# Sixteen transposes of the last pair moved from TensorE to transposing transfers on SyncE's queue

## The chip, the cores and the metric

The kernel runs on one core of one Trainium2 chip. The metric is the device time of one execution in microseconds (us), the median of several runs. Beside the times there is one profiled execution, taken by the hardware profiler. The engines are called PE (TensorE), DVE (VectorE), ACT (ScalarE), POOL (GpSimd) and SP (SyncE, which here only issues transfers).

## The reference

Gated linear attention as a recurrence over time, and then a two-layer MLP with a cosine gate, on its output:

```python
batch, n_heads, seq, head_dim = (4, 8, 768, 48)
for t in range(S):
    state = alpha[:, :, t, :, None] * state + einsum('bhd,bhe->bhde', k[:, :, t], v[:, :, t])
    y[:, :, t] = einsum('bhd,bhde->bhe', q[:, :, t], state)
x = y.transpose(0, 2, 1, 3).reshape(3072, 384)
h = x @ w_in            # 384 -> 2048
out = (h * cos(h)) @ w_out   # 2048 -> 384
```

All inputs and the output are float32; the kernel works in bf16 inside its products.

## The kernel before

The 3072 tokens are cut into twelve "pairs" J = 0..11 of 256 tokens, three for each of the four batches. Within a pair the 128 partitions hold 128 positions, and e = 0, 1 picks the even or the odd token of a position, so each partition has two tokens. The recurrence is computed in chunks of 64 positions: within a chunk as a masked score product, between chunks through a state.

For each pair the attention goes through these steps:

- `load` (L111) brings alpha, k, q and v in, each one transfer issued by SP.
- `ln` (L148), `cums` (L161 to L178) and `exps` (L200, L201) turn alpha into the decays cp and their inverses icp.
- `scale_k` (L206) and `scale_q` (L210) multiply k by icp and q by cp, giving kh and qh in bf16, on POOL for the late pairs. Each head takes 64 columns there, 48 of them used, so that two heads make 128 columns.
- `trans` (L236) transposes kh and qh on PE, in 128x128 blocks of two heads: for each e four blocks of kh and four of qh, so sixteen in a pair. They go to one PSUM tile T_ps per e, and `evict_T` (L242) copies that to the SBUF tile qkT, on DVE.
- `scores` (L252) multiplies, for each e, the transposed k of this e with the transposed q of both e, into two PSUM tiles A_ps. `mask` (L258) on DVE moves them to A_sb.
- `outer` (L270), `add_state` (L284) and `decay_state` (L292) carry the state on.
- `yT` (L329) forms the transposed output from A_sb, v, the state and the transposed q, and `evict_y` (L336) copies it to xT.

The MLP of a pair follows. `mlp1` (L346, the step m1) makes four blocks u of h in PSUM, two buffers of h_ps in turn; `cosine` (L352) on ACT and `gate` (L357) on DVE make gsb from each; `mlp2` (L366, the step m2) makes two halves of the output, each in four parts of four matmuls, and `evict_o` (L371) copies each half out of PSUM. Each half is stored by two transfers (L375), on SP but for the very last, from one of four buffers o_sb.

The order of the work is not that of the loops. Every piece is a `step` with an engine, a length, the steps that it needs, a rank and the buffers that it takes and gives. A planner in the kernel (L516 to L610) plays the steps through with these lengths and writes them out in the order of their planned starts; each engine then executes its own instructions strictly in that order. The lengths in the steps are the planner's numbers and not measurements. The planner also puts matmuls on zeros (`idle`, L384) into early gaps of PE.

The planner has a list DMAT of pairs whose transposes are planned as transfers, as one step per e on an engine "DMA", with a length of its own. It is empty before the change:

```python
if J in DMAT:
    step(("evT", J, e), "DMA", 2.0, [("sk", J, e), ("sq", J, e), ("yT", J - 2)],
         lambda J=J, e=e: trans_dma(J, e), r + RK["trans"], [("qkT", 1)] if e == 0 else [])
```

The step of the scores needs ("evT", J, 0) and ("evT", J, 1) in either form. A step on "DMA" is taken as usable some 2 to 3.5 us after its planned end.

Of the kernel before, what the change touches and what calls it, by code (L numbers as in the profile page):

```python
# [10 lines left out]
BF = mybir.dt.bfloat16  # L11
# [5 lines left out]
def kernel(  # L17
# [10 lines left out]
    nc = tc.nc  # L28
    B, H, S, D = q.shape
    DM, DF = moe_w_in.shape  # L30
    C = 128
# [4 lines left out]
    NP = H // 2  # L36
# [7 lines left out]
    NL, NQ, NV = 4, 3, 3  # L44
    BUF = {"a": 4, "in": 3, "cp": 3, "vb": 3, "qkT": 3, "A": 2, "un": 4, "us": 2, "c": 3, "xT": 3, "g": 4}

    consts = ctx.enter_context(tc.tile_pool(name="consts", bufs=1))
    sb = ctx.enter_context(tc.tile_pool(name="sb", bufs=2))
# [31 lines left out]
    lna_t, qh_t, kh_t, vz_t = [], [], [], []  # L80
    for r in range(NL):
        t = consts.tile([C, 2, H, 64], BF, tag=f"lna{r}", name=f"lna{r}")
        nc.vector.memset(t[:, :, :, D:64], 0.0)
        lna_t.append(t)
    for r in range(NQ):
        t = consts.tile([C, 2, H, 64], BF, tag=f"qh{r}", name=f"qh{r}")
        nc.vector.memset(t[:, :, :, D:64], 0.0)
        qh_t.append(t)
        t = consts.tile([C, 2, H, 64], BF, tag=f"kh{r}", name=f"kh{r}")
        nc.vector.memset(t[:, :, :, D:64], 0.0)  # L90
        kh_t.append(t)
    for r in range(NV):
        t = consts.tile([C, 2, NP, 2, 32], BF, tag=f"vz{r}", name=f"vz{r}")
# [7 lines left out]
    w1 = consts.tile([C, KT, DF], BF, tag="w1", name="w1")  # L101
    w2 = consts.tile([C, NF, DM], BF, tag="w2", name="w2")

    a_sb, kqv, cp_sb, icp_sb, vb_sb, qkT_sb, A_sb, c2_sb = {}, {}, {}, {}, {}, {}, {}, {}
# [88 lines left out]
    def exps(J, e):  # L193
        act_set("exp")
        w = HD + 2 * NP * e
        icp_sb[J, e] = sb.tile([C, HD], FP, tag=f"icp{e}", name="icp", bufs=BUF["cp"])
        if (J, e) not in cp_sb:
            cp_sb[J, e] = sb.tile([C, w], FP, tag=f"cp{e}", name="cp", bufs=BUF["cp"])
        t = cums_ps[J, e] if (J, e) in cums_ps else cp_sb[J, e]
        nc.scalar.activation(out=icp_sb[J, e], in_=t[:, 0:HD], func=AF.Exp, scale=-1.0)  # L200
        nc.scalar.activation(out=cp_sb[J, e], in_=t[:, 0:w], func=AF.Exp)  # L201
# [30 lines left out]
    def trans(J, e):  # L232
        T_ps[J, e] = ps.tile([C, 2 * NP, C], BF, tag="sh", name="T_ps", bufs=3)
        for i, x in ((1, kh_t[J % NQ]), (0, qh_t[J % NQ])):
            for p in range(NP):
                nc.tensor.transpose(T_ps[J, e][:, i * NP + p, :],  # L236
                                    x[:, e, 2 * p : 2 * p + 2, :].rearrange("s h d -> s (h d)"), ident_bf)

    def evict_T(J, e, copy):
        if J not in qkT_sb:  # L240
            qkT_sb[J] = sb.tile([C, 2, 2 * NP, C], BF, tag="qkT", name="qkT", bufs=BUF["qkT"])
        copy(out=qkT_sb[J][:, e], in_=T_ps.pop((J, e)))  # L242
# [145 lines left out]
    steps = {}  # L388

    def step(name, eng, length, deps, fn, rank, take=(), give=()):  # L390
        steps[name] = (eng, length, [d for d in deps if d is not None], fn, rank, take, give)
# [14 lines left out]
    HOLD = 0.29  # L406
    FULL = [0, 1, 2]
    WARM = 5.0
    DMAT = []
    copies = {"DVE": nc.vector.tensor_copy, "ACT": nc.scalar.copy, "POOL": nc.gpsimd.tensor_copy}  # L410
    mults = {"DVE": nc.vector, "POOL": nc.gpsimd}
    blk = {J: n for n, Js in enumerate(BLOCKS) for J in Js}
# [20 lines left out]
    for J in range(NJ):  # L433
# [13 lines left out]
        for e in range(2):  # L447
            if J in FULL:
                src = ("cums", J) if e else ("cums0", J)
            else:  # L450
                src = ("sub", J)
            step(("exps", J, e), "ACTe", 1.0, [src, ("exps", J, 0) if e and J in FULL else None],
                 lambda J=J, e=e: exps(J, e), rb, [], [("h" if J in FULL else "sh", 1)] if e else [])
            eng = SCALE.get((J, "k", e), "POOL")
            step(("sk", J, e), eng, 1.0 if eng == "POOL" else 0.9, [("exps", J, e), ("ld", "k", J)],
                 lambda J=J, e=e, eng=eng: scale_k(J, e, mults[eng]), r + RK["sk"] + e,
                 [("qk", 1)] if e == 0 else [], [("in_k", 1)] if e else [])
            eng = SCALE.get((J, "q", e), "POOL")
            step(("sq", J, e), eng, 1.0 if eng == "POOL" else 0.9, [("exps", J, e), ("ld", "q", J), ("sk", J, 0)],
                 lambda J=J, e=e, eng=eng: scale_q(J, e, mults[eng]), r + RK["sq"] + e, [], [("in_q", 1)] if e else [])  # L460
            eng = EVT.get((J, e), "DVE")
            if J in DMAT:
                step(("evT", J, e), "DMA", 2.0, [("sk", J, e), ("sq", J, e), ("yT", J - 2)],
                     lambda J=J, e=e: trans_dma(J, e), r + RK["trans"], [("qkT", 1)] if e == 0 else [])
            else:
                step(("trans", J, e), "PE", 0.45, [("sk", J, e), ("sq", J, e), ("yT", J - 2) if J > 1 else None],
                     lambda J=J, e=e: trans(J, e), r + RK["trans"], [("sh", 1)])
                step(("evT", J, e), eng, 0.72 if eng == "DVE" else 1.1, [("trans", J, e)],
                     lambda J=J, e=e, eng=eng: evict_T(J, e, copies[eng]), r + RK["evT"],
                     [("qkT", 1)] if e == 0 else [], [("sh", 1)])  # L470
            step(("scores", J, e), "PE", 0.33, [("evT", J, 0), ("evT", J, 1), ("scores", J, 0) if e else None],
                 lambda J=J, e=e: scores(J, e), r + RK["scores"], [("sh", 2)])
            for a in range(2):
                step(("mask", J, e, a), "DVE", 0.69,
                     [("scores", J, e), ("mask", J, e, 0) if a else (("mask", J, 0, 1) if e else None)],
                     lambda J=J, e=e, a=a: mask(J, e, a), r + RK["mask"], [("A", 1)] if a + e == 0 else [], [("sh", 1)])
# [42 lines left out]
    HOP = 0.2  # L519
# [3 lines left out]
    mode, end, order = "e", {}, []  # L523
# [20 lines left out]
    while avail:  # L544
        cands = {}
        cur = undone[0] if undone else []
        for name, dep in avail.items():
            eng, length, deps, fn, rank, take, give = steps[name]
            t = buffers(take)
            if t is None:  # L550
                continue
            t = max(t, dep)
            extra = 0.0
            if eng in ("ACTe", "ACTs"):
                begun = any(("ln", J) in end for J in cur)
                if eng == "ACTe":
                    if name[1] not in cur or (not begun and sins and rank > sins[0]):
                        continue
                    if mode == "s" and not begun:
                        if not all(("ln", J) in avail for J in cur):  # L560
                            continue
                        t = max([t] + [avail["ln", J] - 1.0 for J in cur])
                elif mode == "e" and begun:
                    continue
                if eng[3] != mode:
                    extra = 1.3
            e = eng[:3] if eng[:3] == "ACT" else eng
            cands.setdefault(e, []).append((max(t, free_at[e]), rank, name, extra))

        pick = None  # L570
        for e, cs in cands.items():
            s0 = min(cs)[0]
            c = min((c for c in cs if c[0] <= s0 + (HOLD if c[2][1] in EARLY else NEAR)), key=lambda c: (c[1], c[0]))
            if pick is None or c[0] < pick[0]:
                pick = c + (e,)
        s, rank, name, extra, e = pick
        eng, length, deps, fn, _, take, give = steps[name]
        avail.pop(name)
        if eng in ("ACTe", "ACTs"):
            mode = eng[3]  # L580
        if eng == "PE" and s < WARM:
            length *= 1.9
        end[name] = s + extra + length
        if name[0] == "sin":
            sins.remove(rank)
        if name[0] == "exps":
            n = BLOCKS.index(cur)
            logs_left[n] -= 1
            if logs_left[n] == 0:
                undone.pop(0)  # L590
        free_at[e] = end[name] if e != "X" else 0.0
        for buf, n in take:
            slots[buf][1] += n
        for buf, n in give:
            f, nt, ng = slots[buf]
            for i in range(n):
                f[(ng + i) % len(f)] = end[name]
            slots[buf][2] += n
        for kind in (name, ("start", name)):
            for u in users.get(kind, []):  # L600
                need[u] -= 1
                if need[u] == 0:
                    t = 0.0
                    for d in steps[u][2]:
                        if d[0] != "start":
                            far = steps[d][0][:3] != steps[u][0][:3]
                            t = max(t, end[d] + (HOP if far else 0.0) + ((3.5 if d[1][0] == "w" else 2.0) if steps[d][0] == "DMA" else 0.0))
                    avail[u] = t
        order.append((s, len(order), fn, name))
    assert len(order) == len(steps)  # L610
# [42 lines left out]
```

## Time and profile before

| what | value |
|---|---|
| median of 3 runs | 201.83 us (201.4 to 202.19) |
| the profiled execution | 202.26 us |
| its span, first to last instruction | 200.5 us |
| PE busy | 187.4 us, 93% of the span |
| DVE, ACT, POOL busy | 128.7, 130.2, 92.2 us |
| transposes L236, 192 matmuls | two groups of 96 (kh and qh), 219 ns each in the records, overlapping |
| evictions L242 on DVE | 23, mean 686 ns |
| transfers issued by SP: loads | 48, 384 KB each, 5.3 to 6.2 us to landing (medians of the four kinds) |
| transfers issued by SP: stores | 47, 96 KB each, 2.2 us to landing (median) |

Busy time is the time in which an engine has at least one instruction at work; matmuls are pipelined, so a record of 219 ns does not mean that PE gives one transpose in 219 ns. The chain of work that ended last goes back from the last instruction, at each step to what released it, and so tells which work set the end. On SP the page counts no busy time; its timeline has the instructions that issue transfers, and for how long each held SP.

### The profile page before, as it was taken

The numbers are of one execution on the slowest core, as the hardware profiler recorded it, in microseconds if no ns is written. First come the engines' busy times: TensorE is split into PE (matmuls) and PEld (weight loads), VectorE is DVE, ScalarE is ACT, GpSimd is POOL, SyncE is SP. The second block draws the span as 40 slices with busy tenths as digits, with TensorE's granted clock in tenths as the row PEclk, the third lists the DMA queues.
The fourth block names the chain that finished last, engine by engine and source line by source line (L and its number), as shares of the span: only waits on it lengthen the run. The fifth ranks groups of instructions, "written<-read, shape, count | busy, mean of one in ns | idle before, by whom it ended". The sixth has DMA issues, their size and how long they took to land.

```text
span 200.5 us, 6778 instructions
## 1 busy us (share of the span) xinstructions
PE 187.4 (93%) x2977; PEld 139.0 (69%) x2977; DVE 128.7 (64%) x185; ACT 130.2 (65%) x174; POOL 92.2 (46%) x144
## 2 busy tenths in 40 slices
PE   7889897789999899799999999999999999999990
PEld 7777785566767667568767767777777677687750
DVE  7384585478757756656867776768668578744341
ACT  3521674567796796796887887887878873365520
POOL 4496685138339465749285474165343531000000
PEclk9999999999999999999999999999999999999998
DMA  6999999978996799195819547120110110110203
GB/s 155 261 246 255 258 194 223 208 180 193 264 260 157 165 270 252 38 272 146 207 44 244 129 115 183 23 58 5 43 43 2 41 43 3 39 43 3 67 11 80
DMA packets 57502, 27.18 MB, mean 136 GB/s; under 512 B 50816, under 2 KB 57472, under 8 KB 57472
## 3 DMA queue, kind: packets, MB, share of 16 engines
q1 hardware_dynamic: 53680, 23.50, 50.0%
q0 software_dynamic: 3712, 3.15, 9.8%
q8 instruction: 23, 0.38, 0.8%
q10 hardware_dynamic: 80, 0.10, 0.2%
q14 instruction: 7, 0.06, 0.1%
HBM read 25.17 MB, written 4.72 MB: 149 GB/s over the span
## 4 chain that ended last, share of the span: by engine, by line
PE 61%; DMA 15%; SPq 9%; POOL 6%; issue 3%; ACT 2%; DVE 1%; POOLq 0%; DVEq 0%
PE h_ps L346 24%; PE o_ps L366 22%; SPq L111 9%; DMA k_sb<-in_k_dram 8%; DMA w<-in_moe_w_in_dram 4%; PE y_ps L329 4%; DMA v_sb<-in_v_dram 3%; PE T_ps L236 3%; PE o_last L366 3%; PE A_ps L252 3%; POOL kh L206 2%; POOL qh L210 2%; PE U_ps L270 2%; POOL vz L218 1%; POOL vb L215 1%
## 5 line engine op out<-in xcount | busy, mean ns | idle before, releaser
L357 DVE TENSOR_TENSOR gsb<-h_ps,c_sb 128x1024 bf16<-128x1024 f32 x48 | 58.4, 1221 | 22.4 <-ACT c_sb L352 21.3
L346 PE MATMUL h_ps<-xT,w 128*128 128x256 bf16 x576 | 70.4, 273 | 1.9 <-DMA w<-in_moe_w_in_dram 1.6
L352 ACT ACTIVATE c_sb<-h_ps,halfpi 128x1024 bf16<-128x1024 f32 x48 | 53.2, 1113 | 28.9 <-PE h_ps L346 28.8
L366 PE MATMUL o_ps<-w,gsb 128*128 128x384 bf16 x352 | 65.0, 327 | 1.6 <-ACT o_sb L371 0.6
L346 PEld LDWEIGHTS <-w 128*128 128x128 bf16 x576 | 54.1, 98 | 11.2 <-DMA w<-in_moe_w_in_dram 1.8
L366 PEld LDWEIGHTS <-gsb 128*128 128x128 bf16 x384 | 35.3, 98 | 23.3 <-issue 1.3
L258 DVE TENSOR_TENSOR A_sb<-A_ps,msk 128x512 bf16<-128x512 f32 x48 | 30.8, 685 | 21.0 <-PE A_ps L252 21.0
L206 POOL TENSOR_TENSOR kh<-k_sb,icp 128x384 bf16<-128x384 f32 x23 | 23.0, 999 | 25.3 <-ACT icp L200 20.0
L292 POOL TENSOR_TENSOR un<-us,c 128x384 bf16<-128x384 f32 x20 | 16.7, 833 | 24.9 <-DVE us L284 21.3
L210 POOL TENSOR_TENSOR qh<-q_sb,cp 128x384 bf16<-128x384 f32 x19 | 18.7, 1001 | 0.0
L371 ACT COPY o_sb<-o_ps 128x384 f32<-128x384 f32 x22 | 10.5, 477 | 10.6 <-PE o_ps L366 10.6
L242 DVE COPY qkT<-T_ps 128x1024 bf16<-128x1024 bf16 x23 | 15.0, 686 | 2.3 <-PE T_ps L236 2.0
L154 POOL TENSOR_TENSOR a_sb<-a_sb 128x384 f32<-128x384 f32 x9 | 9.0, 997 | 15.6 <-DMA a_sb<-in_alpha_dram 15.6
L384 PE MATMUL idle_ps<-zeros 128*128 128x128 bf16 x192 | 14.2, 236 | 1.0 <-DVE halfpi L78 1.0
L336 ACT CAST xT<-y_ps 128x384 bf16<-128x384 f32 x22 | 9.5, 481 | 8.5 <-PE y_ps L329 8.5
L384 PEld LDWEIGHTS <-zeros 128*128 128x128 bf16 x192 | 12.6, 107 | 1.3 <-DVE halfpi L78 1.0
L143 ACT ACT_TABLE_LOAD x10 | 12.8, 1283 | 0.9 <-PEq L637 0.7
L148 ACT ACTIVATE lna<-a_sb 128x768 bf16<-128x768 f32 x12 | 10.1, 845 | 4.9 <-DMA a_sb<-in_alpha_dram 4.8
L284 DVE TENSOR_TENSOR us<-U_ps,un 128x384 f32<-128x384 f32 x16 | 8.9, 553 | 6.8 <-PE U_ps L270 4.7
L352 ACT ACT_TABLE_LOAD x10 | 12.8, 1283 | 0.2
L215 POOL CAST vb<-v_sb 128x768 bf16<-128x768 f32 x12 | 9.9, 825 | 5.7 <-PE y_ps L329 4.0
L236 PE MATMUL T_ps<-ident_bf,qh 128*128 128x128 bf16 x96 | 9.3, 219 | 2.8 <-DVE qh L210 1.7
(65 smaller groups left out, 171.6 us busy)
## 6 DMA issues: line engine op xcount, KB each, us to landing
a_sb<-in_alpha_dram SPq DMA_DIRECT2D x12, 384.0 KB, 6.2
k_sb<-in_k_dram SPq DMA_DIRECT2D x12, 384.0 KB, 5.8
v_sb<-in_v_dram SPq DMA_DIRECT2D x12, 384.0 KB, 6.1
q_sb<-in_q_dram SPq DMA_DIRECT2D x12, 384.0 KB, 5.3
out_dram<-o_sb SPq DMA_DIRECT2D x47, 96.0 KB, 2.2
w<-in_moe_w_in_dram POOLq DMA_DIRECT2D x4, 384.0 KB, 8.4
w<-in_moe_w_out_dram POOLq DMA_DIRECT2D x4, 384.0 KB, 8.8
out_dram<-o_sb ACTq DMA_DIRECT2D x1, 96.0 KB, 2.5
```

The source lines that it names most:

```text
L111: nc.sync.dma_start(out=t.rearrange("p h e d -> p h (e d)"), in_=x[b, :, g * T2 : (g + 1) * T2, :].rearrange("h (p e) d -> p h (e d)", e=2),)
L206: eng.tensor_tensor(out=kh_t[J % NQ][:, e, :, 0:D], in0=kqv["k", J][:, :, e], in1=icp, op=ALU.mult)
L210: eng.tensor_tensor(out=qh_t[J % NQ][:, e, :, 0:D], in0=kqv["q", J][:, :, e], in1=cp, op=ALU.mult)
L236: nc.tensor.transpose(T_ps[J, e][:, i * NP + p, :], x[:, e, 2 * p : 2 * p + 2, :].rearrange("s h d -> s (h d)"), ident_bf)
L242: copy(out=qkT_sb[J][:, e], in_=T_ps.pop((J, e)))
L258: nc.vector.tensor_tensor(out=A_sb[J][:, e, a], in0=A_ps[J, e][a], in1=msk[:, e].rearrange("s e2 t -> s (e2 t)").unsqueeze(1).to_broadcast ...
L292: nc.gpsimd.tensor_tensor(out=u, in0=U_sum.pop(n), in1=c2_sb[J][:, :, c].unsqueeze(3).to_broadcast([C, NP, 2, D]), op=ALU.mult)
L346: nc.tensor.matmul(h_ps[J, u][:, f, :], w1[:, kk, ft * C : (ft + 1) * C], xT[J][:, kk, :], start=(kk == 0), stop=(kk == KT - 1))
L352: nc.scalar.activation(out=c_sb[J, u], in_=h_ps[J, u], func=AF.Sin, bias=halfpi, scale=1.0)
L357: nc.vector.tensor_tensor(out=gsb[J][:, u * FW : (u + 1) * FW], in0=h_ps.pop((J, u)), in1=c_sb.pop((J, u)), op=ALU.mult)
L366: nc.tensor.matmul(o_ps[J, c][:, 0:DM], gsb[J][:, ft, c * C : (c + 1) * C], w2[:, ft], start=(ft == 0), stop=(ft == NF - 1))
L384: nc.tensor.matmul(idle_ps[0][:, 0:C], zeros, zeros, start=True, stop=True)
```

## The change

For the last pair, J = 11, the transposes are no longer made by PE and evicted by DVE. SP issues sixteen transfers instead, each of which reads a 128x128 block of kh or qh from SBUF, transposes it, and writes it to its place in qkT in SBUF. The planner's length for such a step goes from 2.0 to 4.0 for each e (eight transfers), and a test of the step's name in the planner is written so that it also works for the step evT.

```diff
+    def trans_dma(J, e):
+        if J not in qkT_sb:
+            qkT_sb[J] = sb.tile([C, 2, 2 * NP, C], BF, tag="qkT", name="qkT", bufs=BUF["qkT"])
+        for i, x in ((1, kh_t[J % NQ]), (0, qh_t[J % NQ])):
+            for p in range(NP):
+                nc.sync.dma_start(out=qkT_sb[J][:, e, i * NP + p, :],
+                                  in_=x[:, e, 2 * p : 2 * p + 2, :].rearrange("s h d -> s (h d)"), transpose=True)
+
...
-    DMAT = []
+    DMAT = [11]
...
             if J in DMAT:
-                step(("evT", J, e), "DMA", 2.0, [("sk", J, e), ("sq", J, e), ("yT", J - 2)],
+                step(("evT", J, e), "DMA", 4.0, [("sk", J, e), ("sq", J, e), ("yT", J - 2)],
                      lambda J=J, e=e: trans_dma(J, e), r + RK["trans"], [("qkT", 1)] if e == 0 else [])
...
-                            t = max(t, end[d] + (HOP if far else 0.0) + ((3.5 if d[1][0] == "w" else 2.0) if steps[d][0] == "DMA" else 0.0))
+                            t = max(t, end[d] + (HOP if far else 0.0) + ((3.5 if d[1] in ("w1", "w2") else 2.0) if steps[d][0] == "DMA" else 0.0))
```

In the order that results, the sixteen transfers stand on SP behind the stores of pair 8's second half and ahead of all stores of pairs 9, 10 and 11. On PE the sixteen transposes are gone, and the order from there to the end is another: the first two blocks of pair 10's m1 come before pair 11's scores (one of them did before), and the last block of pair 11's m1 comes after two m2 parts of that pair instead of before all of them. POOL's order is unchanged.

## The prediction

> **What bounds the kernel now.** I read the busy times first, then the chain of work that ended last, then what the sync queue (SP) does, because the change takes work from TensorE and gives it to SP.
>
> ```profile
> PE 187.4 (93%) x2977; PEld 139.0 (69%) x2977; DVE 128.7 (64%) x185; ACT 130.2 (65%) x174; POOL 92.2 (46%) x144
> ```
>
> TensorE is busy 93% of the span and no other engine is over 65%. By stage, in windows of 10 us (columns: busy time of each engine, granted clock, DMA share, GB/s):
>
> ```profile
> 160.00:170.00 10.00, 10.00 (x185) 7.59 (x174) 7.56 (x9) 5.76 (x8) 2.77 (x4) 1.00 0.10 23
> 170.00:180.00 10.00, 10.00 (x184) 7.32 (x183) 6.44 (x8) 5.16 (x7) 0.00 (x0) 1.00 0.17 41
> 180.00:190.00 10.00, 10.00 (x81) 7.51 (x79) 3.67 (x3) 4.88 (x6) 0.00 (x0) 1.00 0.12 29
> ```
>
> In the stage of the change TensorE has no idle time, its clock is granted in full, and the DMA engines are busy 10 to 17%. The chain says the same (start, duration, engine, tile):
>
> ```profile
> 168.61 0.89 PE T_ps L236 x16
> 169.50 0.65 PE o_ps L366 x4
> 170.15 1.31 PE h_ps L346 x12
> 171.46 0.35 PE A_ps L252 x16
> ...
> 177.59 1.11 PE y_ps L329 x88
> ...
> 190.58 5.21 PE o_last L366 x32
> 195.82 0.56 DVE o_sb L371
> ```
>
> From 113 us to 195.82 us the chain is TensorE work without a gap. The sixteen transposes are 0.89 us of it, and the scores (A_ps), which need them, come 1.96 us later. Anything taken off TensorE here shortens the run, and any wait put in front of it lengthens the run by its full length.
>
> Last SP, by its timeline and by its two lines (duration of issuing one transfer, minimum, median and maximum in ns):
>
> ```profile
> 161.60 0.47 SPq L375 DMA_DIRECT2D out_dram<-o_sb  x1
> 162.12 0.59 SPq L375 DMA_DIRECT2D out_dram<-o_sb  x1
> ```
> ```profile
> 159.98 1.95 POOL L210 TENSOR_TENSOR qh<-q_sb,cp 128x384 bf16<-128x384 f32 x2
> ```
> ```profile
> L111 SPq DMA_DIRECT2D q_sb<-in_q_dram x12: 373/712/4103, 4.3 to 120.0; - x12
> L375 SPq DMA_DIRECT2D out_dram<-o_sb x47: 466/588/1512, 44.5 to 196.9; - x47
> DMA to landing us min/median/max: 2.1/2.2/6.4
> ```
>
> SP is never done with a transfer in no time: 0.37 us at the least, 0.59 us in the middle for a store, 0.71 us for a load of q. A store lands 2.2 us after its issue.
>
> **The change, part by part.** *Removed from TensorE*: pair 11's sixteen transposes, 0.89 us on the chain. With nothing in their place the run is 0.89 us shorter. *Removed from VectorE*: two evictions (L242, 686 ns each), 1.4 us. VectorE has 2.4 us idle in 160 to 170, and the chain doesn't touch it until 195.82: nothing. The freed PSUM buffer is waited for by nothing on the chain: nothing.
>
> *Moved*: the planner now places a second block of pair 10's first MLP product ahead of pair 11's scores, where one stood before. TensorE's queue after the m2 parts of pair 9 that end at 168.61 reads: m1 block 0 of pair 10 (1.31), the last m2 part of pair 9's first half (0.65), m1 block 1 of pair 10 (1.31), scores. So TensorE stands at the scores at 168.61 + 1.31 + 0.65 + 1.31 = 171.88 us. That second block came after the scores before, so this moves work and adds none. I followed buffers to the end: each PSUM buffer of the first product is free before its block starts, and the last gate (about 2.4 us after the last m1 block, from a cosine of 1.11 and a gate of 1.23) is covered by four m2 parts (4 x 0.65 = 2.6 us), where six covered it before. That margin is 0.2 us; without it, the end loses those tenths.
>
> *Added to SP*: sixteen transposing transfers, behind the second pair-8 store, which SP has issued at 162.12 + 0.59 = 162.71. Their last source, qh, is done at 161.93, so from there they are paced by SP alone. They go in the order kh, qh of the even positions, then kh, qh of the odd ones; the first scores need all of qh, so they end with the sixteenth transfer. Between two issues SP leaves 0.05 us (162.07 to 162.12). With a pitch p from one issue to the next, the last starts at 162.76 + 15p and lands 2.2 us later. [...]
>
> No transposing transfer and no transfer from SBUF to SBUF is in this trace, so p is bounded. Below: the shortest issue, 0.373 + 0.05 = 0.42 us; the last lands at 171.3, before 171.88, and costs nothing. Above: a queue that takes each only after the one before has landed, p = 2.2; the last lands at 198.0. In between: a store (64 rows of 1536 bytes), 0.59 + 0.05 = 0.64; a load of q (1024 pieces of 384 bytes), 0.71 + 0.05 = 0.76; loads issued one behind another into a full queue, 1.48 (7.25 to 8.73 us). A transpose reads 128 rows of 256 bytes and writes 128 others, more pieces than a store and fewer than a load, and it does more than a copy. I take the median load of q, p = 0.76.
>
> [...]
>
> *The sum*: the last lands at 162.76 + 15 x 0.76 + 2.2 = 176.4, so TensorE waits 176.4 - 171.88 = 4.5 us at the scores. Three quarters of the scores (0.26 us) run in that wait as their transfers land. 4.5 - 0.26 - 0.89 = +3.4 us. Behind the waiting scores stand the rest of pair 9's second product, all of the MLP of pairs 10 and 11 and pair 11's yT; none can pass, as TensorE works in order. On SP the stores of pairs 9 to 11 are queued behind the transposes: the first would go at about 175 instead of 170.7, and its buffer, one of four, is wanted again only near 195. Nothing. The DMA engines, 10 to 17% busy, have room for 16 x 32 KB.
>
> The profiled execution took 202.26 us (span 200.5, 1.8 us around it); 202.26 + 3.4 = 205.7. The median shown is 201.83, 0.4 lower, so I forecast 205.2.
>
> **The clock.** A long wait costs more than itself:
>
> ```profile
> 1.00 3.91 PE L384 MATMUL idle_ps<-zeros 128*128 128x128 bf16 x35 [1.00 <-DVE halfpi L78]
> 6.20 2.00 PE L384 MATMUL idle_ps<-zeros 128*128 128x128 bf16 x33
> 199.00:200.00 1.00, 0.00 (x0) 0.00 (x0) 0.00 (x0) 0.00 (x0) 0.00 (x0) 0.72 0.00 0
> ```
>
> The same idle matmul takes 112 ns (3.91/35) in the first 3.9 us and 61 ns (2.00/33) afterwards. After TensorE's last matmul at 195.8 the granted clock falls to a half at about 199.4 (a mean of 0.72 in that window), after some 3.6 us of idleness. A wait over 3.6 us without a matmul thus costs about 3.9 x (1 - 61/112) = 1.8 us more. At p = 0.76 the first group of scores can start at 162.76 + 12 x 0.76 + 2.2 = 174.1, after 2.2 us: no fall. From p = 0.88 on there is one.
>
> **The rivals.**
> *Hidden.* If p is at most (171.88 - 2.2 - 162.76)/15 = 0.46 us, all land in time and 0.89 us is won: 200.9 us. Up to p = 0.54 it isn't slower than before. For it: the shortest load (0.373) and the shortest store (0.466) are at about that. Against it: the two stores just before took 0.47 and 0.59.
> *Issue far dearer.* If a transpose holds SP as long as a load into a full queue, p = 1.48, the last lands at 187.2, TensorE waits 15.3 us and its clock falls: 15.3 - 0.26 - 0.89 + 1.8 = +16, 217.8 us. For it: SP did take 1.44 us per transfer from 4 to 10 us. Against it: then the DMA engines were full, here they are nearly idle.
> [...]
> *One at a time.* p = 2.2: 26.1 us of wait, 26.1 - 1.15 + 1.8 = +26.7, 228.5 us. [...]
>
> **How the numbers follow.** Half a per cent, 1.0 us, is about what a measurement of this kernel can tell from no change. The forecast, with p from 0.6 to 1.05 us and its own range from 202.8 to 211 us, gets 0.37; hidden or nearly so gets 0.22; issue far dearer 0.27; one at a time or worse 0.14. A wait for the transfers is thus likely at 0.78: slower 0.78. A hidden transfer wins at most 0.89 us, under the bound unless the run falls well: same 0.17, faster 0.05. The range goes from 200.8, the hidden case, to 220, where p is 1.6, and leaves out 0.14 above and a little below.
>
> **What the profile after would show.** Sixteen transposing issues on SP from about 162.8; their pitch is p, the number that everything hangs on. No T_ps on TensorE and no L242-like eviction for pair 11. The first scores of pair 11 reached at about 171.9 and held by a DMA for some 2 us, then going in four groups one pitch apart; everything behind shifted by about 3.4 us and no further gap to the end. With a clock row below 1.00 after the wait, the dearer case is in. I am wrong if SP's pitch is under 0.54 us, if landing takes much more than 2.2 us, or if a gap stands elsewhere, above all at the last gate.

## The result, and the profile after

The changed kernel takes 216.15 us in the median of four runs (215.02 to 217.34), the kernel before 201.74 us beside it: a ratio of 1.0714, 95% interval 1.0649 to 1.0779. It is 7% slower. The profiled execution took 216.57 us with a span of 214.8 us, 14.3 us more than the one before.

TensorE's share of busy time fell from 93% to 88% with nearly the same busy time, so it now waits. From the page of the changed kernel:

```profile
PE 188.8 (88%) x2961; PEld 138.8 (65%) x2961; DVE 127.5 (59%) x183; ACT 130.2 (61%) x174; POOL 92.2 (43%) x144
```

Where, the windows of the stage show (length, busy time of PE, its weight loads, DVE, ACT and POOL, granted clock, DMA share, GB/s):

```profile
170.00:172.00 2.00, 2.00 (x19) 1.59 (x18) 0.29 (x1) 1.44 (x2) 0.00 (x0) 1.00 0.16 32
172.00:174.00 2.00, 0.48 (x5) 0.29 (x3) 0.93 (x1) 1.16 (x2) 0.00 (x0) 1.00 0.09 17
174.00:176.00 2.00, 0.00 (x0) 0.00 (x0) 0.00 (x0) 0.00 (x0) 0.00 (x0) 0.81 0.16 33
...
186.00:188.00 2.00, 2.00 (x9) 0.97 (x8) 1.96 (x3) 0.00 (x0) 0.00 (x0) 0.50 0.33 78
188.00:190.00 2.00, 2.00 (x25) 0.96 (x23) 1.28 (x3) 0.00 (x0) 0.00 (x0) 0.78 0.00 0
```

TensorE runs out of work at 172.48 us, and from 173.6, when ScalarE's last cosine is done, until the first scores at 181.8 nothing computes on any engine. The DMA engines are busy 9 to 17% of the time, and the clock falls to a half (0.50 in the mean of 176 to 188), which it still is when TensorE starts again. The timeline of SP over the same stretch (start, duration, count in the merged row) tells who was at work:

```profile
163.49 5.71 SPq L244 DMA_TRANSPOSE qkT<-kh  x4
169.31 5.01 SPq L244 DMA_TRANSPOSE qkT<-qh  x4
174.36 5.05 SPq L244 DMA_TRANSPOSE qkT<-kh  x4
179.51 5.00 SPq L244 DMA_TRANSPOSE qkT<-qh  x4
```

SP issues transposes back to back for 21 us. By the line's own answer one issue holds SP for 1.23 us (minimum, median, maximum in ns) and lands 2.3 us after its start:

```profile
L244 SPq DMA_TRANSPOSE qkT<-kh x8: 1176/1230/1947, 163.5 to 178.2; - x8
L244 SPq DMA_TRANSPOSE qkT<-qh x8: 1172/1230/1242, 169.3 to 183.3; - x8
...
DMA to landing us min/median/max: 2.3/2.3/3.8
```

The scores of pair 11 wait for them, in four groups, as TensorE's timeline shows (in brackets the idle time before and what ended it), and the chain of work from there to the end is late by that much:

```profile
181.83 0.32 PE L260 MATMUL A_ps<-qkT 48*64 48x128 bf16 x4 [9.35 <-DMA qkT<-qh]
183.10 0.32 PE L260 MATMUL A_ps<-qkT 48*64 48x128 bf16 x4 [0.94 <-DMA qkT<-qh]
184.43 0.32 PE L260 MATMUL A_ps<-qkT 48*64 48x128 bf16 x4 [1.01 <-DMA qkT<-qh]
185.69 0.32 PE L260 MATMUL A_ps<-qkT 48*64 48x128 bf16 x4 [0.94 <-DMA qkT<-qh]
```
```profile
183.28 2.37 DMA qkT<-qh
...
185.69 0.32 PE A_ps L260 x3
186.00 2.67 PE o_ps L374 x8
188.68 0.45 PE A_ps L260 x14
189.13 1.41 PE o_ps L374 x8
```

The first eight m2 matmuls behind the wait take 2.67 us, the next eight, once the clock is back, 1.41.

The 14.3 us add up. TensorE reaches the scores at 172.48 (181.83 less the 9.35 of idle time), 0.60 later than the 171.88 worked out from the run before, since this run was already 0.6 us later at 158 us, ahead of the change. The last group of scores starts at 185.69, 13.21 later. The half clock costs 1.44 (a run below). Off go 0.89 for the transposes and 0.26 for three groups of scores done in the wait; 0.2 is not assigned. 0.60 + 13.21 + 1.44 - 0.89 - 0.26 + 0.2 = 14.3.

### The profile page after: what moved, and what is told of

It reads as the page before. It is cut to its first block, busy times and chain, and to the rows that moved or that the text cites. A ratio compares the mean times of both kernels' runs of the same rounds, so it can differ in the third digit from the quotient of the medians.

```text
span 214.8 us, 6764 instructions
## 1 busy us (share of the span) xinstructions
PE 188.8 (88%) x2961; PEld 138.8 (65%) x2961; DVE 127.5 (59%) x183; ACT 130.2 (61%) x174; POOL 92.2 (43%) x144
## 4 chain that ended last, share of the span: by engine, by line
PE 49%; SPq 17%; DMA 15%; POOL 6%; issue 4%; ACT 4%; DVE 2%; POOLq 0%; DVEq 0%; ACTq 0%
PE o_ps L374 19%; PE h_ps L354 18%; SPq L244 9%; SPq L111 8%; DMA v_sb<-in_v_dram 5%; DMA w<-in_moe_w_in_dram 5%; DMA k_sb<-in_k_dram 5%; PE y_ps L337 4%; PE o_last L374 2%; PE T_ps L236 2%; PE A_ps L260 2%; POOL kh L206 2%; POOL qh L210 2%; ACT c_sb L360 2%; DMA qkT<-qh 1%
## 5 line engine op out<-in xcount | busy, mean ns | idle before, releaser
L374 PE MATMUL o_ps<-w,gsb 128*128 128x384 bf16 x352 | 65.9, 331 | 2.9 <-DMA w<-in_moe_w_out_dram 1.9
L260 PE MATMUL A_ps<-qkT 48*64 48x128 bf16 x384 | 11.0, 227 | 12.7 <-DMA qkT<-qh 12.2
L260 PEld LDWEIGHTS <-qkT 48*64 48x64 bf16 x384 | 6.9, 108 | 19.4 <-issue 18.7
L250 DVE COPY qkT<-T_ps 128x1024 bf16<-128x1024 bf16 x21 | 13.7, 686 | 2.0 <-PE T_ps L236 1.7
```

The costliest lines, as they stand in the source:

```text
L260: nc.tensor.matmul(A_ps[J, e][a][m, p, :].rearrange("s (e2 t) -> s e2 t", e2=2), qkT[r, e, NP + p, m], qkT[r, :, p, m], start=True, stop=True)
L374: nc.tensor.matmul(o_ps[J, c][:, 0:DM], gsb[J][:, ft, c * C : (c + 1) * C], w2[:, ft], start=(ft == 0), stop=(ft == NF - 1))
```

## The experiments

The question was no longer where the time went but why an issue costs 1.23 us and not the 0.37 to 0.71 of the stores and loads: because these transfers are SBUF to SBUF, because they transpose, by size or by count; and what the fallen clock adds. The theory after the result: SP pays a fixed price per transposing instruction. Its rivals: a price of the kind of transfer, or a price per row or block. That SP is held until the transpose before it is done can be left aside: the first of the sixteen, with none ahead of it, held SP for 1.18 us.

**Plain copies in the same places.**

```diff
-                                  in_=x[:, e, 2 * p : 2 * p + 2, :].rearrange("s h d -> s (h d)"), transpose=True)
+                                  in_=x[:, e, 2 * p : 2 * p + 2, :].rearrange("s h d -> s (h d)"))
```

> The sixteen transfers of the changed kernel stay where they are, with the same blocks, but copy without transposing, so pair 11's scores are computed from untransposed blocks. Theory A, transposing is what makes an issue dear (pitch 1.32 us in the profile of the change): plain copies go at the pitch of a store, about 0.64 us, the last lands at about 175.3 us, TensorE waits some 3 us, the clock stays up, about 204.4 us; down to 201 us if the pitch is that of the shortest issues, 0.42. Rival B, any transfer from SBUF to SBUF by this queue costs 1.3 us: 216 us as the changed kernel.

206.01 us in one run. The line's answer for these copies:

```profile
L244 SPq DMA_DIRECT2D qkT<-kh x8: 498/600/609, 162.4 to 170.5; - x8
L244 SPq DMA_DIRECT2D qkT<-qh x8: 546/600/1701, 165.0 to 173.1; - x8
```

One issue takes as long as a store's, as theory A has it: 0.60 us, and it is the transposing that doubles it. The time came out 1.6 us above the 204.4 expected, and the windows show why:

```profile
172.00:175.40 3.40, 1.15 (x18) 0.60 (x18) 0.11 (x1) 0.58 (x1) 0.00 (x0) 1.00 0.27 61
175.50:178.80 3.30, 3.30 (x26) 1.45 (x24) 2.69 (x4) 0.00 (x0) 0.00 (x0) 0.50 0.13 31
178.90:182.00 3.10, 3.10 (x27) 2.49 (x26) 0.71 (x2) 1.15 (x2) 0.00 (x0) 1.00 0.10 23
```

The clock fell to 0.50 although TensorE's longest gap was 1.65 us; in the 3.4 us ahead of the fall it had 1.15 us of work. Behind the wait the first eight m2 matmuls took 2.46 us instead of 1.41 and the next eight 1.71.

**Four blocks in one instruction.**

```diff
-            for p in range(NP):
-                nc.sync.dma_start(out=qkT_sb[J][:, e, i * NP + p, :],
-                                  in_=x[:, e, 2 * p : 2 * p + 2, :].rearrange("s h d -> s (h d)"), transpose=True)
+            nc.sync.dma_start(out=qkT_sb[J][:, e, i * NP : (i + 1) * NP, :],
+                              in_=x[:, e].rearrange("s h d -> s (h d)"), transpose=True)
```

> Four transposing transfers of 128 rows x 512 columns (four blocks each) in place of sixteen of 128 x 128; everything else as in the changed kernel. Theory A1, SP pays about 1.2 us per transposing instruction whatever its size: the last of four starts at about 167.4 and lands at 169.8 us, before TensorE is at the scores at 172.4; no wait, about 200.9 us, 0.4% under the kernel before. Theory A2, SP pays per block or row of the transpose: a pitch of about 4.9 us, the last lands at about 183 to 185 us as now, 214 to 216 us. In between (a fixed part of 0.4 and 0.8 per block): pitch 3.6, the last lands at about 177, 206 us.

201.42 us against 202.41 beside it, a ratio of 0.9971 (0.9938 to 1.0005). SP's timeline, and the chain around the scores:

```profile
162.22 1.29 SPq L243 DMA_TRANSPOSE qkT<-kh  x1
163.62 1.21 SPq L243 DMA_TRANSPOSE qkT<-qh  x1
164.88 2.40 SPq L243 DMA_TRANSPOSE qkT<-kh  x1
167.37 1.22 SPq L243 DMA_TRANSPOSE qkT<-qh  x1
```
```profile
169.90 1.31 PE h_ps L353 x12
171.21 0.35 PE A_ps L259 x16
```

A transfer of four blocks holds SP as long as one of one block. The wait is gone: the scores follow the m1 block without a gap. This is theory A1. (The last section has more on the one issue of 2.40 us.)

**Half the rows.** The same sixteen instructions, each for 64 of the 128 rows.

```diff
+            nc.gpsimd.memset(qkT_sb[J][:, e, i * NP : (i + 1) * NP, HC:C], 0.0)
...
-                nc.sync.dma_start(out=qkT_sb[J][:, e, i * NP + p, :],
-                                  in_=x[:, e, 2 * p : 2 * p + 2, :].rearrange("s h d -> s (h d)"), transpose=True)
+                nc.sync.dma_start(out=qkT_sb[J][:, e, i * NP + p, 0:HC],
+                                  in_=x[0:HC, e, 2 * p : 2 * p + 2, :].rearrange("s h d -> s (h d)"), transpose=True)
```

> Sixteen transposing transfers of 64 rows x 128 columns in place of 128 x 128; the other 64 columns of each block of pair 11's transposed q and k are set to zero by POOL, which is idle there, so half of that computation is left out. Theory A1, a fixed price per instruction: pitch 1.3 us as now, 216 us. Theory A2, a price per row or block: the pitch falls towards 0.65 to 0.85 us, the last lands at about 174 to 178 us, 203 to 207 us.

215.67 us in one run, with the issues no shorter:

```profile
L245 SPq DMA_TRANSPOSE qkT<-kh x8: 1172/1226/2264, 162.2 to 177.1; - x8
L245 SPq DMA_TRANSPOSE qkT<-qh x8: 1167/1226/1226, 168.3 to 182.2; - x8
```

With 64, 128 or 512 columns of output an issue takes 1.2 us: the price is per instruction.

**Two blocks in one instruction**, eight transfers, to see whether the prediction's sum gives the time once its pitch is right.

```diff
-            for p in range(NP):
-                nc.sync.dma_start(out=qkT_sb[J][:, e, i * NP + p, :],
-                                  in_=x[:, e, 2 * p : 2 * p + 2, :].rearrange("s h d -> s (h d)"), transpose=True)
+            for p in range(0, NP, 2):
+                nc.sync.dma_start(out=qkT_sb[J][:, e, i * NP + p : i * NP + p + 2, :],
+                                  in_=x[:, e, 2 * p : 2 * p + 4, :].rearrange("s h d -> s (h d)"), transpose=True)
```

> Eight transposing transfers of 128 rows x 256 columns in the changed order. With a fixed price per instruction, pitch 1.27 us (plus once some 0.7 us more, as in every run so far near 166 us): the last starts at about 172.4 to 173.1 and lands at 174.8 to 175.5 us, where TensorE stands at the scores at 172.3 us. The wait is 2.5 to 3.2 us, 10 us less than with sixteen, and the clock falls for at most one stretch of 3.4 us: 203.5 to 206 us. If the price grew with the size beyond some point, later: 206 to 216 us.

205.53 us, a ratio of 1.0181 (1.0126 to 1.0236), inside the expectation. The last transfer was issued at 173.21 and landed 2.38 later, and the second group of scores started at 175.63. With 256 columns an issue took 1.24 us. The clock held here (1.00 in the mean of 172 to 176, with 1.05 us of work), although TensorE stood idle for 1.99 us ahead of the first group of scores, longer than the longest gap with plain copies; so the length of a gap alone does not say whether the clock falls. The chain shows 1.41 us for the m2 behind the wait:

```profile
173.21 2.38 DMA qkT<-qh
...
175.63 0.31 PE A_ps L260 x8
175.94 1.41 PE o_ps L374 x8
```

**Zero matmuls in the wait**, to price the clock. First 205 of them, then 250:

```diff
+    wait_at = next(s for s, _, _, name in order if name == ("scores", NJ - 1, 0))
+
+    def warm():
+        t = ps.tile([C, 512], FP, tag="o_ps", name="warm_ps", bufs=1)
+        for _ in range(205):
+            nc.tensor.matmul(t[:, 0:C], zeros, zeros, start=True, stop=True)
+
+    order.append((wait_at - 0.001, len(order), warm, ("warm",)))
```

> 205 matmuls on zeros are put on TensorE ahead of pair 11's scores, to run inside the wait (12.5 us of them at 61 ns); nothing else changes. If the fall of the clock in the wait costs what the profile shows behind it (eight m2 matmuls took 2.67 us at half clock against 1.41), the clock stays at 1.00, the wait itself is as long as before and the time falls by about 1.4 us, to 214.8 us; the prediction had put 1.8 us on it. If the half clock costs nothing of its own: 216 us.

219.1 us, and not 214.8: a miss. The zero matmuls took 57 ns and not 61, so they ended at 183.2, the last transfer landed late (3.7 us after its issue), and the clock fell at 186 (a mean of 0.52 in 186 to 188), just as the work began again:

```profile
186.78 0.32 PE A_ps L260 x4
187.10 2.67 PE o_ps L374 x8
...
190.34 2.67 PE o_ps L374 x8
```

Now both m2 groups ran at half clock. With 250:

> As the experiment with 205 zero matmuls in the wait, but 250 of them: at the 57 ns that they took there they run from 171.6 to about 185.9 us, up to the landing of the last transfer, where the 205 had ended 3.5 us before it and the clock fell all the same. If the fall of the clock is a cost of its own: the clock stays at 1.00 behind the wait, the eight m2 matmuls there take 1.4 instead of 2.7 us, and with up to 0.8 us lost to zero matmuls that run past the landing the time is 214.8 to 215.6 us. If the slow m2 matmuls have another cause, they still take 2.7 us: 216.5 us or more.

```profile
186.42 0.25 PE A_ps L260 x4
186.67 1.41 PE o_ps L374 x8
```

The clock stayed up (1.00 in 172 to 186 and in 186 to 190) and the m2 behind the wait took 1.41. From the last group of scores to the end of the last copy out of PSUM it is 23.54 us here (186.42 to 209.96) and 24.98 in the changed kernel (185.69 to 210.67): the fallen clock costs 1.44 us. The time was 215.77 us, hardly less than 216.15 and just above the expectation, because in this run the last transfer also landed late, at 186.4: two more of its issues took 1.86 and 2.23 us.

**The planner told the truth.** One number: the length of a step of eight transfers, 4.0 in the change, set to the 10.2 us that they take.

```diff
-                step(("evT", J, e), "DMA", 4.0, [("sk", J, e), ("sq", J, e), ("yT", J - 2)],
+                step(("evT", J, e), "DMA", 10.2, [("sk", J, e), ("sq", J, e), ("yT", J - 2)],
```

> The changed kernel with one number changed: the planner's length for eight transposing transfers is 10.2 (8 x 1.27 measured) instead of 4.0. The planner then puts the rest of pair 9's and all of pair 10's MLP ahead of pair 11's scores, so TensorE reaches them at about 182.8 us, close to the landing of the last transfer at 185.7. The wait falls from 13.3 to about 3 us, but pair 11's chain (scores, masks, yT, copies, MLP), which the MLP of pair 10 covered, then stands alone, some 18 us from scores to the last matmul: 208 to 211 us. If the wait alone were the loss, it would be 216.2 - 10 = 206 us or less.

213.59 us in one run, above the expected 208 to 211. The chain:

```profile
187.49 0.37 PE A_ps L260 x4
187.86 0.69 DVE A_sb L266
...
190.01 1.78 PE y_ps L337 x74
...
192.70 5.25 PE h_ps L354 x24
```

The wait was shortened as planned, but two stores, now between the transposes on SP, and a later start put the landing at 187.5. From there pair 11's attention runs alone, step by step over TensorE and VectorE, with the clock at a half again from 187.5 (means of 0.94 in 184 to 188 and 0.50 in 188 to 192): two blocks of m1 took 5.25 us where they took 2.62 in the changed kernel. The loss is not only the wait in front of TensorE: the last pair has no other work to cover a late start, and the clock fell in the waits.

**Merged transfers in the order of before.** To see whether the other order on TensorE had a part in what the four transfers won, and then for nine pairs.

```diff
...
-    DMAT = []
+    DMAT = [11]
...
+    for J in DMAT:
+        for z, (s, k, fn, name) in enumerate(order):
+            if name[:2] in (("trans", J), ("evT", J)):
+                order[z] = (s, k, lambda: None, name)
+        for e in range(2):
+            order.append((end["sq", J, e], len(order), lambda J=J, e=e: trans_dma(J, e), ("dma",)))
```

> The order of the kernel before on every engine, with pair 11's transposes and their two evictions taken out and four merged transposing transfers put on SP right behind the scalings of q (two for each e). If the 0.89 us of transposes is all that the change can win and the planner's other order wins nothing: 0.9 us under the kernel before, as the merged version in the changed order. If the other order has a part in what that version won: less than that, the same as the kernel before.

202.14 us, ratio 1.0003 (0.9972 to 1.0034): the same as before; 0.9 us less was to be expected if the other order had no part. In its profiled execution the chain has a piece that the kernel before has not, ahead of the last m2 part of pair 9's first half: with the transposes gone, TensorE reaches it before its gate is done.

```profile
164.42 1.43 PE h_ps L353 x12
...
165.87 1.12 ACT c_sb L359
...
167.02 1.24 DVE gsb L364
168.25 0.05 issue
168.30 0.82 PE o_ps L373 x4
```

The transposes had covered that gate; without them 0.52 of their 0.89 us becomes a wait of TensorE. In the changed order a block of m1 covers it instead. So by the chain the other order did have a part. The times alone do not show it: the intervals of the two merged versions overlap.

> The same for pairs 3 to 11: the order of before, nine pairs' transposes and evictions taken out, 36 merged transposing transfers on SP at about 1.25 us each. If TensorE stays the bound and each pair's transfers land before its scores (they have some 9 us from the last scaling of q, and need 5 us of SP and 2.5 to land): 9 x 0.89 = 8.0 us less, 193.5 to 194.5 us. If SP, which waits in order for the evictions of the stores and the buffers of the loads, holds the transfers up, TensorE waits at the scores in every pair: anything from 196 up to over 205 us.

With DMAT = list(range(3, 12)) the four executions took 215.6 to 221.6 us, above the 205 us named for the dear case. The longest waits on SP, and the one on TensorE, in the profiled execution (221.6 us):

```profile
SPq L382 <- ACT o_sb L378: 44.9, 12, 8.2
SPq L111 <- POOL kh L206: 12.7, 3, 6.8
...
PE A_ps L259 <- DMA qkT<-qh: 10.6, 3, 4.1
```

On SP a transfer goes behind those ahead of it in the order, as in the changed kernel, where the stores behind the transposes went from 184.61, and in the kernel before from 170.69; so here a transpose stands behind stores that wait for ACT (44.9 us in total) and loads that wait for POOL (12.7 us). These waits are not new (in the kernel before, the stores waited 77.9 us for ACT), but no transpose stood behind them there. The loads of alpha stand behind the transposes in turn, and POOL waited 30.6 us for them, against 15.6 us in the kernel before. That these two make the loss is an argument from the waits; how the 14 to 20 us divide wasn't measured.

**The four transfers again**, in more rounds on another chip.

> The version with four merged transfers again, in more rounds: 0.89 us of TensorE's chain less than the kernel before and no wait, so a ratio of about 0.9956; if the 0.29% of the first measurement was chance, 1.000.

201.57 against 202.06, ratio 0.997 (0.9936 to 1.0004). Each interval alone takes in 1; both put the gain at 0.3%. Taking the two as independent, with a half width of 0.0034/1.41, gives 0.9946 to 0.9994. That is the best version found, and it is less than the half per cent that one such measurement can tell.

## Why the prediction was wrong

- *What bounds the kernel* held. TensorE bound this stage, and a wait in front of the scores came through to the end in full, apart from the 0.89 and 0.26 us named.
- *The place* held: sixteen issues on SP from 163.5 (162.8 forecast), the scores reached at 172.5 (171.9), held in four groups one pitch apart. The landing, 2.37 us for the last transfer, was as taken (2.2). The stores behind the transposes were late by 14 us (184.61 instead of 170.69) and nothing waited for them.
- *The step that failed is the pitch p*: 0.76 us was taken from the median load of q, and it was (183.28 - 163.49)/15 = 1.32 us: issues of 1.23, gaps of 0.04 to 0.11, and one issue of 1.95. With 1.32 the same sum gives 162.76 + 19.8 + 2.2 = 184.8, a wait of 12.9 us, and with its 1.8 us for the clock 201.83 + 13.5 = 215.4 us, 0.7 from the measured time. So the mechanism was right and one term was too small. What put it wrong was the argument from pieces: between a store's 64 rows and a load's 1024 pieces I placed a transpose near the load. The runs show that neither rows nor blocks matter (64, 128, 256 or 512 columns out: 1.2 us), and that transposing as such doubles the 0.60 us of the same plain copy (to landing it is 2.3 us against 1.8). Without the one issue of 1.95 us the pitch is 1.27.
- *The rival* "issue far dearer" (p = 1.48, 217.8 us, chance 0.27) is the one that came in, though for another reason than its own: a load took 1.44 us with the DMA engines full (a share of 1.27 in 4 to 10 us of the kernel before), a transpose 1.23 with them 9 to 17% busy. The direction, slower at 0.78, was right; the size, +3.4 us, was a quarter of the measured 14.4.
- *The clock* fell, as the long-wait case had it, and cost 1.44 us (1.8 estimated). The condition was wrong: I asked for 3.6 us without a matmul, and with plain copies the clock fell after a longest gap of 1.65 us, while it held with eight transfers through one of 1.99.
- *The 0.89 us* to be won is what the merged version comes near to: its chain has no transposes and no wait, and two measurements put it 0.3% below the kernel before. In the order of before it was not won, as a gate stood behind it; the margins that I followed to the end of the changed order held.

## What to carry to other kernels

Price a transfer by how long it holds the queue that issues it, per instruction, and multiply by the count before comparing with the engine that it relieves: sixteen issues at 1.23 us replaced 0.89 us of TensorE. If a transfer must be used, let one instruction do more (with up to 512 columns of output it held SP for 1.2 us here), and leave the queue free in front of it. Work of the last stage is a bad place for a long latency, since little is left behind it to fill the wait.

## What was not expected of the hardware

- A transposing issue held SP for 1.2 us with 64 to 512 columns of output, and in the changed kernel the DMA engines were idle for most of one (164.72 to 165.93 us). In windows between two bursts and in the next one, their share is 0.01 and 0.53:

```profile
164.95:165.93 0.98, 0.98 (x15) 0.67 (x13) 0.33 (x1) 0.49 (x1) 0.00 (x0) 1.00 0.01 0
165.93:166.22 0.29, 0.29 (x4) 0.26 (x3) 0.27 (x1) 0.29 (x1) 0.00 (x0) 1.00 0.53 113
```

- From its fall to its return the half clock lasted 13.64 us in the changed kernel, 6.84 us in the run with 205 zero matmuls and 3.3 to 3.5 us with plain copies. In the changed kernel the means of 0.81 in 174 to 176 and 0.78 in 188 to 190 put its fall at 175.24 and its return at 188.88. In the run with 205 zero matmuls means of 0.52 in 186 to 188 and 0.77 in 192 to 194 put them at 186.08 and 192.92. With plain copies the clock was 1.00 up to 175.4, 0.50 from 175.5 to 178.8 and 1.00 again from 178.9. The first length is twice the second, and that is about twice the third; no run shows why. Nor does one show what holds the clock: with plain copies it fell behind 3.4 us with 1.15 us of matmuls, and with eight transfers it held through 4 us with 1.05.
- In the changed kernel and in seven runs with transfers in that place one issue near 165 to 168 us took 1.7 to 2.4 us instead of 0.6 or 1.2, by time and not by number (the third of sixteen, the sixth plain copy, the third of four). In the changed kernel, where it ran from 165.98 to 167.93 us, the DMA queues show what else went on then: one transfer on a queue that the profile calls "instruction" (23 of them and 0.38 MB in the whole execution, so about 16 KB each):

```profile
q8 instruction: 1, 0.02, 3.5%
```

  From 167.97 to 184.51, where the other thirteen of its issues took 1.17 to 1.24 us, there is none. Of the other runs only the counts of the whole execution are shown: 25 in the run with 250 zero matmuls, which had two more long issues, and 23 with the planner's true length, which had one. So the two stand together in the changed kernel, which is not a tested cause; and not every such transfer made an issue longer: two stores beside one that started at 184.25 us in the kernel before, from 184.92, took 0.47 and 0.59 us.
